# A pair with a nearly empty second block becomes a single with a small block beside it

## The chip, the cores and the metric

One core of a Trainium2 chip runs the whole program in one launch. The metric is device time in microseconds (us), median of the runs. Engines: PE (matrix), DVE (vector), ACT (activation), POOL (GpSimd; it issues the indirect gathers and scatters), SP (issues the plain DMAs). PE's weight loads are listed as PEld.

## The reference, cut to what matters

```
a = attention(q, k, v)              # 4 batches, 8 heads, 768 positions, window plus block summaries
x = a as 3072 tokens of 512 numbers
g_idx = argmax(x @ w_group)         # 4 groups
e_idx = argmax(xg @ w_expert[g])    # 4 experts in the group: 16 experts, one for each token
for each expert with tokens:
    h  = relu(xe @ w1[g, e])        # 512 -> 1024
    ye = h @ w2[g, e]               # 1024 -> 512
    out[tokens] = (g_weight * e_weight)[:, None] * ye
```

Counted from the reference on the given inputs, experts 0 to 15 get 0, 203, 922, 118, 0, 1445, 0, 4, 1, 0, 0, 0, 0, 379, 0 and 0 tokens. In blocks of 128: expert 1 two (128 and 75 tokens), expert 2 eight (the last has 26), expert 3 one (118), expert 5 twelve (the last has 37), experts 7 and 8 one each (4 tokens and 1), expert 13 three (the last has 123).

## The kernel before, in words

**Stages.** Attention runs first and writes x to DRAM. Beside it the Router works out each token's expert and place. Four full blocks of the expert that leads after two batches ("first", here expert 5) run while the router finishes; their work is `first`. All other blocks become units, and the unit tables are made on the chip by `units`, `unit_rows` and `unit_slots` while `first` runs: `units` turns the counts per expert into the number of pairs, singles ("ones") and tiny units and their first row; `unit_rows` writes the table of the unit's expert (SP reads it to load weights); `unit_slots` builds one-hot columns (`eq`, `bo`), multiplies them on PE, and writes the table of token numbers, `t_unit_gather`, which POOL's gathers read.

**A planner sets the order** of the router's instructions among the blocks of `first`. It keeps a modelled PE clock and a modelled DVE clock; each DVE instruction is charged 85 ns (`VECTOR_NS`) and 1 ns a column, a 256-column matmul 107 ns. After each step of `first` (12 matmuls of stage 1, 6 of stage 2) it appends router instructions until the DVE clock is past the PE clock. `pause` holds a matmul back until the PE clock is ahead of the DVE clock by so many ns. What isn't appended when the last half block of `first` is to begin (tag "units") is appended there, ahead of that half block. Engines then run their queues in order.

**A unit** has two stages: x (high and low part) times w1, relu, times w2 (high and low part); three matmuls for each product in split precision. ACT writes the high parts (L1032), DVE the low ones. A `pair` has two blocks of 128 tokens of one expert and one set of weights (4 MB, SP, L1018). A `one` has one block, and a `tiny` unit at most 32 tokens, in plain fp32 on the raw weights in four column strips. Two pairs are certain, further pairs are nested `If`s (L1302). Then come the ones, nested (L1311), and behind each `one(i)` the `tiny(i)` if there is one (L1315). For the counts above that makes ten pairs, two ones (experts 3 and 13) and two tiny units (7 and 8).

**Around a one.** At its start POOL gathers the tokens of tiny unit i+1 and of the one after next, then drains; SP loads the next one's weights and those of the tiny unit. `x_t_tiny(i)` (L1208) transposes the tiny tokens in the second stage of `one(i)`: PE executes it in order. Scatters to `out` go out in order on POOL, each waiting for the one before it.

**A skipped `If`.** Each engine branches by itself. Where the body is skipped, an engine that has instructions in it runs one semaphore instruction in its place, which waits until the engine's own earlier instructions are done and raises its semaphore by what the body would have raised.

Of the kernel before, what the change touches and what calls it, by code (L numbers as in the profile page):

```python
# [8 lines left out]
F32 = mybir.dt.float32  # L9
F32R = mybir.dt.float32r  # L10
BF16 = mybir.dt.bfloat16
I32 = mybir.dt.int32
# [8 lines left out]
P = 128  # L21
# [19 lines left out]
NONE = E  # L41
TINY = 32
NTINY = E // 2
SLOTS = 2 * NPAIR + NONE + NTINY
# [25 lines left out]
AHEAD, LATE_AHEAD, SLOT_AHEAD, VECTOR_NS = 300, 1500, 800, 85  # L70
# [64 lines left out]
class Router:  # L135
# [3 lines left out]
    def __init__(self, tc, pool, ps, ident):  # L139
# [16 lines left out]
        for name, rows, n in (("first", 1, 1), ("unit", 32, 3), ("count", 1, 3), ("next", 32, 1)):  # L156
            t[name] = pool.tile([rows, n], I32, name="t_" + name)
# [216 lines left out]
    def slots(self, name, col, nt, step, c0):  # L374
# [5 lines left out]
        eqs = [self.tile("eq_%s%d" % (name, j0), step, n) for j0 in groups]  # L380

        def columns(values):
# [3 lines left out]
            for j0, eq in zip(groups, eqs):  # L386
# [8 lines left out]
                yield from self.pause(SLOT_AHEAD)  # L395
# [49 lines left out]
    def units(self):  # L445
# [18 lines left out]
        un = self.tile("un", 3, E)  # L464
        V.tensor_copy(out=un, in_=bi)
        yield

        V.scalar_tensor_tensor(out=un[:, 2], in0=un[:, 2], scalar=1.0, in1=un[:, 1], op0=ALU.is_equal, op1=ALU.mult)
        yield
        start = self.start = self.tile("ustart", 3, E)  # L470
        for a, z in ((0, 2), (2, 3)):
            before = self.tile("look", 2, E, E)[:, 0:z - a]
            V.tensor_tensor(out=before, in0=self.lower[:, None].broadcast_to([P, z - a, E, E]),
                            in1=un[:, a:z, None, :].broadcast_to([P, z - a, E, E]), op=ALU.mult)
            yield
            V.reduce_sum(out=start[:, a:z], in_=before, axis=AX.X)
            yield
        end = self.end = self.tile("uend", 3, E)
        V.tensor_tensor(out=end, in0=start, in1=un, op=ALU.add)
        yield  # L480


        large = self.tile("ularge", 1)
        V.tensor_tensor(out=large, in0=end[:, 1, E - 1:E], in1=end[:, 2, E - 1:E], op=ALU.subtract)
        yield
        V.scalar_tensor_tensor(out=un[:, 2], in0=start[:, 2], scalar=large, in1=un[:, 2], op0=ALU.is_lt, op1=ALU.mult)
        yield
        below = self.tile("ubelow", E)
        V.tensor_scalar(out=below, in0=start[:, 2], scalar1=large, scalar2=None, op0=ALU.min)
# [3 lines left out]
        V.tensor_tensor(out=start[:, 1], in0=start[:, 1], in1=below, op=ALU.subtract)  # L493
        yield
        V.tensor_tensor(out=end[:, 1:3], in0=start[:, 1:3], in1=un[:, 1:3], op=ALU.add)
# [7 lines left out]
        V.tensor_tensor(out=ut[:, 2], in0=start[:, 2], in1=start[:, 1], op=ALU.subtract)  # L503
        yield
        V.scalar_tensor_tensor(out=ut[:, 2], in0=ut[:, 2], scalar=float(NONE), in1=un[:, 2], op0=ALU.add, op1=ALU.mult)
        yield
        V.tensor_tensor(out=ut[:, 2], in0=ut[:, 2], in1=start[:, 1], op=ALU.add)
# [437 lines left out]
class Experts:  # L945
# [11 lines left out]
    def tiles(self, pool, early):  # L957
# [17 lines left out]
        else:  # L975
# [6 lines left out]
            self.xTt, self.wt = pool.tile([P, KC, TINY], F32, name="xt"), pool.tile([P, 1], F32, name="wt")  # L982
# [11 lines left out]
    def col(self, row, half=0):  # L994
        name, i = row
        if name == "first":
            return name, i
        return "unit", dict(unit=2 * i + half, one=2 * NPAIR + i, tiny=2 * NPAIR + NONE + i)[name]
# [121 lines left out]
    def pair(self, i):  # L1120
# [39 lines left out]
    def one(self, i):  # L1160
# [10 lines left out]

        def h_t(n):
# [10 lines left out]
        if 0 < i < NTINY:  # L1183
            for which in range(2):
                self.load_w(("tiny", i), which, self.n_tiny > i)
        for n in range(2):
# [11 lines left out]
            self.nc.scalar.activation(out=self.xg2[0][:, n], in_=hp, func=AF.Relu)  # L1198
        load(1)
# [245 lines left out]
```

## Time and profile before

| what | value |
|---|---|
| time, median of 3 runs | 524.16 us (523.22 to 525.19) |
| the profiled execution's own time | 524.9 us |
| its span, first to last instruction | 523.1 us |
| PE busy / PE weight loads busy | 94% / 80% |
| DVE / ACT / POOL busy | 69% / 61% / 23% |
| granted PE clock, mean | 0.989 |
| DMA, mean over the span | 204 GB/s |

Busy shares are averages over stages with different limits: attention up to about 190 us, `first` and the tables up to about 241 us, pairs up to 478 us, then ones and tiny units to 515 us. In a timeline row the first number is the start, the second the time in us, and in brackets stands how long the engine was idle before it and what ended that.

### The profile page before, as it was taken

How to read it: one execution, taken by the hardware profiler on the slowest of the kernel's cores; microseconds unless marked ns; L12 is line 12 of the kernel's file. 1: busy time of each engine (PE TensorE's matmuls, PEld its weight loads, DVE VectorE, ACT ScalarE, POOL GpSimd, SP SyncE). 2: the span in 40 equal slices, each digit the busy share in tenths (PEclk: the TensorE clock that was granted, in tenths of full speed). 3: DMA queues.
4: the chain of work that ended last, by engine and by line, in shares of the span. 5: the costliest groups of instructions: out<-in, count | busy, mean ns of one | idle time of the engine just before them, and what ended most of it. 6: DMA issues, size and time to landing. Idle time of an engine off the chain costs nothing.

```text
span 523.1 us, 13329 instructions
## 1 busy us (share of the span) xinstructions
PE 493.3 (94%) x4966; PEld 418.1 (80%) x4966; DVE 359.7 (69%) x1090; ACT 316.8 (61%) x595; POOL 121.1 (23%) x200
## 2 busy tenths in 40 slices
PE   7799999999999789989999999999999999999993
PEld 4677767776777688969898989899898989897782
DVE  7787899888887878876755547473746546473782
ACT  5599888888989642216645546463645546474681
POOL 7322113111313400045020202022121302023222
PEclk9799999999999999999999999999999999999998
DMA  9999766967757530196996665655566666653890
GB/s 169 181 185 179 159 150 186 182 140 212 167 136 254 173 113 21 48 366 214 404 370 243 243 234 196 250 222 186 200 222 230 244 236 202 256 203 134 283 355 29
DMA packets 72501, 106.95 MB, mean 204 GB/s; under 512 B 40286, under 2 KB 40366, under 8 KB 68576
## 3 DMA queue, kind: packets, MB, share of 16 engines
q1 hardware_dynamic: 67456, 90.98, 59.6%
q0 software_dynamic: 4960, 14.92, 7.8%
q8 instruction: 43, 0.70, 0.6%
q14 instruction: 42, 0.34, 0.3%
HBM read 97.49 MB, written 13.24 MB: 212 GB/s over the span
## 4 chain that ended last, share of the span: by engine, by line
PE 55%; issue 16%; DVE 13%; DMA 10%; ACT 2%; POOL 2%; POOLq 1%; ACTq 0%; DVEq 0%
PE ps_s L120 32%; PE ps_av L120 11%; PE ps_tr L120 11%; DMA out_dram<-y,t_unit_scatter 4%; DVE ss L794 3%; DMA x_dram<-xt 2%; DVE ks L774 2%; DMA xg<-x_dram,t_first_gather 1%; DVE kw L763 1%; DMA xd<-x_dram,t_unit_gather 1%; ACT kw L763 1%; PE ps_lg L658 1%; DVE kw L771 1%; POOLq L1181 1%; POOL out_dram L1078 1%
## 5 line engine op out<-in xcount | busy, mean ns | idle before, releaser
L120 DVE TENSOR_TENSOR w2l<-w2r,w2h 128x1024 fp32r<-128x1024 f32 x52 | 63.4, 1226 | 77.2 <-ACT w2h L1032 76.8
L120 PE MATMUL ps_s<-xT,w1h 128*128 128x256 f32 x448 | 83.6, 285 | 0.0
L120 PEld LDWEIGHTS ps_s<-xT,w1h 128*128 128x128 f32 x448 | 70.8, 192 | 0.9 <-issue 0.6
L1078 POOL DMA_INDIRECT out_dram<-y,t_unit_scatter x24 | 25.8, 1074 | 195.8 <-ACT y L1073 110.3
L120 PE MATMUL ps_s<-xT,w1l 128*128 128x256 f32 x224 | 63.4, 283 | 0.0
L803 ACT ACTIVATE pr<-ss,nm 128x120 f32<-128x120 f32 x192 | 60.1, 387 | 4.7 <-DVE nm L794 4.3
L1116 ACT ACTIVATE hTh<-ps_s 128x512 fp32r<-128x512 f32 x48 | 28.7, 597 | 56.4 <-PE ps_s L120 35.9
L737 POOL COPY va<-vr 24x256 f32<-24x256 f32 x96 | 34.7, 405 | 121.3 <-DVE vr L734 114.4
L120 DVE TENSOR_TENSOR w1l<-w1r,w1h 128x1024 fp32r<-128x1024 f32 x52 | 60.4, 1219 | 3.1 <-ACT w1h L1032 3.1
L120 PE MATMUL ps_s<-ohr,w1h 128*128 128x256 f32 x320 | 59.0, 283 | 0.0
L1032 ACT CAST w2h<-w2r 128x1024 fp32r<-128x1024 f32 x52 | 53.7, 1041 | 1.2 <-DVE lg L864 0.6
L120 DVE SCALAR_TENSOR_TENSOR hTl<-ps_s,hTh 128x512 fp32r<-128x512 f32 x48 | 33.1, 690 | 26.8 <-ACT hTh L1116 26.0
L1032 ACT CAST w1h<-w1r 128x1024 fp32r<-128x1024 f32 x52 | 50.7, 1050 | 0.0
L120 PEld LDWEIGHTS ps_s<-ohr,w1h 128*128 128x128 f32 x320 | 49.9, 188 | 0.2
L794 DVE CUSTOM_DVE_ANT_0 ss<-mask,ps_s 128x120 f32<-128x120 f32 x192 | 42.1, 274 | 4.4 <-PE ps_s L120 3.7
L120 PE MATMUL ps_s<-ohr,w1l 128*128 128x256 f32 x160 | 45.0, 281 | 0.0
L120 PE MATMUL ps_s<-kw,qt 64*64 64x120 f32 x768 | 38.0, 279 | 5.7 <-DVE nm L794 4.6
L120 PEld LDWEIGHTS ps_s<-xT,w1l 128*128 128x128 f32 x224 | 43.0, 192 | 0.3
L120 PE MATMUL ps_s<-w2h,hTh 128*128 128x512 f32 x104 | 41.7, 401 | 0.0
L120 PE MATMUL ps_av<-w2h,hTh 128*128 128x512 f32 x104 | 41.6, 400 | 0.0
L120 PE MATMUL ps_av<-w2l,hTh 128*128 128x512 f32 x104 | 41.1, 395 | 0.0
L120 PE MATMUL ps_s<-w2h,hTl 128*128 128x512 f32 x104 | 41.1, 395 | 0.0
(270 smaller groups left out, 1017.8 us busy)
## 6 DMA issues: line engine op xcount, KB each, us to landing
w2r<-in_moe_w_dram SPq DMA_DIRECT2D x32, 1024.0 KB, 5.3
w1r<-in_moe_w_dram SPq DMA_DIRECT2D x30, 1024.0 KB, 8.6
kn<-in_k_dram SPq DMA_DIRECT2D x16, 384.0 KB
qn<-in_q_dram SPq DMA_DIRECT2D x16, 384.0 KB, 5.6
va<-in_v_dram SPq DMA_DIRECT2D x32, 192.0 KB, 4.0
x_dram<-xt SPq DMA_DIRECT2D x12, 512.0 KB, 4.2
va<-in_v_dram SPq DMA_DIRECT2D x64, 44.0 KB, 5.3
w_first<-in_moe_w_dram SPq DMA_DIRECT2D x2, 1024.0 KB, 5.1
```

The lines of the kernel that those rows point to most:

```text
L120: return f(*args, **kw)
L658: nc.tensor.matmul(out=t, lhsT=zero, rhs=zero[:, None, :].broadcast_to([P, 4, P]), start=True, stop=True)
L737: nc.gpsimd.tensor_copy(out=va[KW:NC, i:i + n, :, 0:D], in_=vr[KW:NC].broadcast_to([NBLK, n, 2, D]))
L763: (nc.scalar.copy if j == 0 or h and idx in ACT_K1 else V.tensor_copy)(out=out[:, j], in_=tv.rearrange("p i t r -> p t r i"))
L771: V.tensor_copy(out=kw[:, 1:NQT, before], in_=kw[:, 0:NQT - 1, QT - PAD:QT])
L774: V.reduce_max(out=ks, axis=AX.X, in_=kw[:, :, 0:QT].rearrange("p t (a k) -> p t a k", k=BLOCK))
L794: V.tensor_tensor_reduce(out=ss[:, u], in0=mask[:, 1 if t == 0 else 2 if t == NQT - 2 else 0], in1=sp[h][:, j], scale=1.0, scalar=3.4e38, ...
L803: nc.scalar.activation(out=pr[:, i, 0:NC], in_=sp[:, i], func=AF.Exp, bias=nm[:, i:i + 1], scale=-1.0)
L1032: self.nc.scalar.copy(out=h, in_=src)
L1078: self.nc.gpsimd.indirect_dma_start(out=self.out, out_offset=bass.IndirectOffsetOnAxis(ap=self.tabs[name, "scatter"][0:y.shape[0], col:col ...
L1116: nc.scalar.activation(out=th[:, js], in_=hp, func=AF.Relu)
L1181: self.nc.gpsimd.drain()
```

## The change

A pair whose second block has at most 32 tokens is no longer a pair. It is listed as a one, behind the ones that have tiny units, and its second block as a small block `i` beside `one(i)`, which uses that one's raw weights. `tiny` is cut in two, `tiny1` (through h) and `tiny2`; beside a one, `tiny1` stands at its start and `tiny2` between its stages, each under `If`s. At most 4 units are tiny and at most 4 beside. For the counts above expert 2's fourth pair (128 and 26 tokens) qualifies: nine pairs, three ones (experts 3, 13 and 2), two tiny units, one small block beside `one(2)`.

```diff
-AHEAD, LATE_AHEAD, SLOT_AHEAD, VECTOR_NS = 300, 1500, 800, 85
+AHEAD, LATE_AHEAD, SLOT_AHEAD, WEIGHT_AHEAD, VECTOR_NS = 300, 1500, 800, 3000, 85
...
-                yield from self.pause(SLOT_AHEAD)
+                yield from self.pause(SLOT_AHEAD if values[0] is self.tok1 else WEIGHT_AHEAD)
...
     def units(self):
...
-        for a, z in ((0, 2), (2, 3)):
-            before = self.tile("look", 2, E, E)[:, 0:z - a]
-            V.tensor_tensor(out=before, ...)          # 128x512, then 128x256
-            V.reduce_sum(out=start[:, a:z], in_=before, axis=AX.X)
+        # the four counts packed into one number, 5 bits each (4 instructions)
+        V.tensor_tensor(out=before, in0=self.lower, in1=packed[:, 1:2].broadcast_to([P, E, E]), op=ALU.mult)
+        V.reduce_sum(out=packed[:, 0], in_=before, axis=AX.X)
+        # ... unpacked (4 instructions), caps, starts and ends by some 30 small ones
...
     def unit_rows(self):
-        V.tensor_copy(out=self.tabs["count"], in_=self.end[0:1, :, E - 1])
+        V.reduce_max(out=cnt[:, 0:3], in_=self.end[0:1], axis=AX.X)
+        V.tensor_copy(out=cnt[:, 3:4], in_=self.n_small[0:1])
+        V.tensor_copy(out=self.tabs["count"], in_=cnt)
...
     def pair(self, i):
                 elif i == 0 and part == 0:
                     self.x_t_one(0)
+                    self.gather(("tiny", 0), self.xg1[0][0:TINY])
+                elif i == 1 and part == 0:
+                    self.x_t_tiny(0)
...
     def one(self, i):
+        def beside(work):
+            if i < NTINY:
+                with self.tc.If(self.n_small > i):
+                    if i < NTINY - NBESIDE:
+                        with self.tc.If(self.n_tiny <= i):
+                            work()
+                    else:
+                        work()
...
-        for t in ((0, 1) if i == 0 else (i + 1,)):
-            if t < NTINY:
-                self.gather(("tiny", t), self.xg2[1][0:TINY, t % 2])
+        beside(lambda: self.tiny1(i, ("one", i)))
+        if i + 1 < NTINY:
+            self.gather(("tiny", i + 1), self.xg2[1][0:TINY, 0])
         self.gather_one(i + 2)
         self.nc.gpsimd.drain()
         load(0)
...
+        beside(lambda: self.tiny2(i, ("one", i)))
         load(1)
         for part, _ in enumerate(self.stage2(...)):
...
-            if part == 1 and i < NTINY:
-                self.x_t_tiny(i)
+            if part == 1 and i + 1 < NTINY:
+                self.x_t_tiny(i + 1)
...
     def tiny(self, i):
+        self.tiny1(i, ("tiny", i))
+        self.tiny2(i, ("tiny", i))
```

So the tokens of tiny unit i+1 are gathered at the start of `one(i)` and transposed in its second stage; before, a whole one lay between. Tiles of the small blocks move into the router's `eq` tiles, and `wt` gets two buffers.

## Rows read from the trace of the kernel before

**Rows 1.** The page: busy time by engine; the chain that ended last, by engine

```profile
PE 493.3 (94%) x4966; PEld 418.1 (80%) x4966; DVE 359.7 (69%) x1090; ACT 316.8 (61%) x595; POOL 121.1 (23%) x200
...
PE 55%; issue 16%; DVE 13%; DMA 10%; ACT 2%; POOL 2%; POOLq 1%; ACTq 0%; DVEq 0%
```

**Rows 2.** Busy time in stretches (start:end, us): two pairs, one(0), tiny(0), one(1)

```profile
283.24:306.93 23.69, 23.69 (x154) 21.49 (x153) 13.51 (x15) 12.36 (x16) 4.28 (x4) 1.00 0.60 222
306.93:330.49 23.56, 23.56 (x153) 21.37 (x153) 13.49 (x15) 12.37 (x16) 4.22 (x4) 1.00 0.62 224
...
478.74:492.26 13.52, 13.52 (x64) 10.68 (x65) 9.97 (x11) 10.41 (x13) 4.70 (x4) 1.00 0.93 330
492.26:496.83 4.57, 4.42 (x132) 3.71 (x131) 2.08 (x4) 1.23 (x3) 2.36 (x5) 1.00 0.43 119
496.83:510.26 13.43, 13.43 (x66) 10.66 (x65) 10.72 (x13) 11.16 (x15) 3.27 (x3) 1.00 0.92 348
```

**Rows 3.** PE's timeline where x_t_tiny(0) stands in one(0)

```profile
488.67 0.66 PE L120 MATMUL ps_tr<-ident,ohr 32*128 32x32 f32 x4
```

**Rows 4.** DVE's timeline while the tables are made

```profile
207.52 0.68 DVE L120 TENSOR_TENSOR look<-lower,un 128x512 f32<-128x512 f32 x1
...
213.00 0.69 DVE L120 SCALAR_TENSOR_TENSOR hTl<-ps_s,hTh 128x512 fp32r<-128x512 f32 x1 [2.23 <-ACT hTh L1116]
...
214.78 0.17 DVE L120 SCALAR_TENSOR_TENSOR ut<-ut,un 128x16 f32<-128x16 f32 x1
214.99 0.18 DVE L120 TENSOR_TENSOR ut<-ut,ustart 128x16 f32<-128x16 f32 x1
...
218.42 0.16 DVE L120 CAST t_unit<-uex 32x3 int32<-32x3 f32 x1
...
227.89 0.22 DVE L120 TENSOR_SCALAR t_unit_gather<-ps_lg 128x62 uint32<-128x62 f32 x1 [1.37 <-PE ps_lg L120]
```

**Rows 5.** POOL's timeline: the first gather of unit 0

```profile
228.38 1.22 POOL L1039 DMA_INDIRECT xd<-x_dram,t_unit_gather  x1 [16.93 <-DVE t_unit_gather L120]
```

**Rows 6.** PE's timeline: the transposes of unit 0's tokens

```profile
235.68 1.23 PE L120 MATMUL ps_tr<-ident,xd 128*128 128x128 f32 x8 [1.25 <-DMA xd<-x_dram,t_unit_gather]
```

**Rows 7.** PE's timeline: from the last pair into one(0)

```profile
477.43 0.39 PE L120 MATMUL ps_s<-w2h,hTl 128*128 128x512 f32 x1
478.74 0.50 PE L120 MATMUL ps_s<-w1h,xs 128*128 128x512 f32 x1 [0.91 <-ACT y L1073]
```

**Rows 8.** Line 1302 from 470 to 479 us: ns min/median/max, first and last start

```profile
L1302 PEldq COMPARE_BRANCH  x2: 193/2005/3817, 473.5 to 478.0; - x2
...
L1302 PEldq EVENT_SEMAPHORE  x1: 51/51/51, 477.9 to 477.9; - x1
```

**Rows 9.** Line 1315 in the whole span, the same columns

```profile
L1315 PEldq COMPARE_BRANCH  x4: 65/124/191, 488.8 to 514.1; - x4
```

**Rows 10.** ACT's timeline: tiny(0)'s output

```profile
496.92 0.74 ACT L1253 ACTIVATE y<-ps_lg,wt 32x128 f32<-32x128 f32 x2 [1.33 <-PE ps_tr L120]
```

**Rows 11.** SP's timeline: weight loads for unit 0 and in one(1)

```profile
219.76 0.99 SPq L1018 DMA_DIRECT2D w1r<-in_moe_w_dram  x2
...
493.95 2.24 SPq L1018 DMA_DIRECT2D w1r<-in_moe_w_dram  x4
```

**Rows 12.** Stretches of 2 us in one(1); the last number is the GB/s moved

```profile
501.00:503.00 2.00, 2.00 (x14) 1.78 (x13) 1.61 (x3) 1.78 (x3) 0.14 (x1) 1.00 0.98 409
...
509.00:511.00 2.00, 2.00 (x34) 1.49 (x36) 2.00 (x4) 1.33 (x2) 0.00 (x0) 1.00 0.16 51
```

**Rows 13.** POOL's timeline: gather of tiny(2) in one(1); the last scatter

```profile
504.08 1.32 POOL L1039 DMA_INDIRECT ohr<-x_dram,t_unit_gather  x1 [0.30 <-issue]
...
516.84 0.89 POOL L1078 DMA_INDIRECT out_dram<-y,t_unit_scatter  x1 [3.14 <-DMA out_dram<-y,t_unit_scatter]
```

**Rows 14.** Line 1039 from 503 to 512 us

```profile
DMA to landing us min/median/max: 5.4/5.7/6.0
```

**Rows 15.** PE's timeline: last matmuls of the program

```profile
514.55 0.28 PE L120 MATMUL ps_lg<-w2r,xd 128*32 128x128 f32 x2
```

More of the change, by code (lines that the diff above doesn't have):

```diff
@@ L43 @@
 NTINY = E // 2
+NBESIDE = NTINY // 2
 SLOTS = 2 * NPAIR + NONE + NTINY
@@ L153, in __init__ @@
         t = self.tabs = {}
-        for name, rows, n in (("first", 1, 1), ("unit", 32, 3), ("count", 1, 3), ("next", 32, 1)):
+        for name, rows, n in (("first", 1, 1), ("unit", 32, 3), ("count", 1, 4), ("next", 32, 1)):
             t[name] = pool.tile([rows, n], I32, name="t_" + name)
@@ L379, in slots @@
         groups = range(0, nt, step)
-        eqs = [self.tile("eq_%s%d" % (name, j0), step, n) for j0 in groups]
+        eqs = self.eqs = [self.tile("eq_%s%d" % (name, j0), step, n) for j0 in groups]
         def columns(values):
@@ new lines, in units @@
+        yield
+        V.tensor_tensor(out=packed[:, 1], in0=packed[:, 0], in1=packed[:, 1], op=ALU.add)
+        yield
+        whole = self.tile("uwhole", 2, E, dt=I32)
+        V.tensor_copy(out=whole, in_=packed)
+        yield
+        field = self.tile("ufield", 4, 2, E, dt=I32)
+        for i in range(4):
+            V.tensor_scalar(out=field[:, i], in0=whole, scalar1=5 * i, scalar2=31, op0=ALU.arith_shift_right, op1=ALU.bitwise_and)
+            yield
+        sf = field.bitcast(F32)
+        V.tensor_copy(out=sf, in_=field)
@@ L478, in units @@
+        yield
+        small = self.n_small = self.tile("unsmall", 1)
+        V.tensor_tensor(out=small, in0=na, in1=nb, op=ALU.add)
+        yield
+        start = self.start = self.tile("ustart", 3, E)
         end = self.end = self.tile("uend", 3, E)
-        V.tensor_tensor(out=end, in0=start, in1=un, op=ALU.add)
+        V.scalar_tensor_tensor(out=un[:, 3], in0=s_b, scalar=float(NBESIDE), in1=un[:, 3], op0=ALU.is_lt, op1=ALU.mult)
         yield
-        large = self.tile("ularge", 1)
-        V.tensor_tensor(out=large, in0=end[:, 1, E - 1:E], in1=end[:, 2, E - 1:E], op=ALU.subtract)
+        V.scalar_tensor_tensor(out=un[:, 2], in0=s_a, scalar=cap, in1=un[:, 2], op0=ALU.is_lt, op1=ALU.mult)
@@ new lines, in units @@
+        yield
+        V.tensor_tensor(out=start[:, 1], in0=s_o, in1=start[:, 2], op=ALU.subtract)
+        yield
+        V.tensor_tensor(out=un[:, 0], in0=un[:, 0], in1=un[:, 3], op=ALU.subtract)
+        yield
+        rest = self.tile("urest", 1, E)
+        V.tensor_scalar(out=rest[:, 0], in0=start[:, 1], scalar1=na, scalar2=nb, op0=ALU.is_ge, op1=ALU.mult)
+        yield
+        V.tensor_tensor(out=start[:, 1], in0=start[:, 1], in1=rest[:, 0], op=ALU.add)
+        yield
+        V.scalar_tensor_tensor(out=rest[:, 0], in0=s_b, scalar=na, in1=start[:, 1], op0=ALU.add, op1=ALU.subtract)
@@ L490, in units @@
+        yield
+        V.tensor_tensor(out=rest[:, 0], in0=rest[:, 0], in1=un[:, 3], op=ALU.mult)
+        yield
+        V.tensor_tensor(out=start[:, 1], in0=start[:, 1], in1=rest[:, 0], op=ALU.add)
         yield
@@ L492, in units @@
         yield
-        V.tensor_tensor(out=start[:, 1], in0=start[:, 1], in1=below, op=ALU.subtract)
+        V.tensor_tensor(out=un[:, 1], in0=un[:, 1], in1=un[:, 3], op=ALU.add)
         yield
-        V.tensor_tensor(out=end[:, 1:3], in0=start[:, 1:3], in1=un[:, 1:3], op=ALU.add)
+        V.tensor_tensor(out=end, in0=start, in1=un[:, 0:3], op=ALU.add)
         yield
@@ L997, in col @@
             return name, i
-        return "unit", dict(unit=2 * i + half, one=2 * NPAIR + i, tiny=2 * NPAIR + NONE + i)[name]
+        return "unit", dict(unit=2 * i + half, one=2 * NPAIR + min(2 * i, i + NTINY), tiny=2 * NPAIR + 2 * i + 1)[name]
     def bank(self, name, i):
```

106 lines of the change are left out of this document (72 added, 34 removed).

## The prediction

> **What bounds the kernel now.** I read the busy shares and the chain first [rows 1]: PE is busy 94% of the span and holds 55% of the chain, and the chain names lines, not stages. So I went to busy time by stretch [rows 2]: in a pair PE is busy for all of its 23.69 or 23.56 us while DVE and ACT need 13.5 and 12.4, so a pair is worth its PE time, 23.62 us, and everything else in it is hidden. A one is full of PE work too, 13.52 and 13.43 us, but DMA is at 330 to 348 GB/s there against 222 in a pair, and a tiny unit adds 4.57 us. Two places are bound otherwise. Ahead of pair 0, PE idles 1.25 us until unit 0's gathered tokens land [rows 6], and that gather hangs on the token table that DVE finishes at 228.1 us [rows 4, 5]; a later table is a later pair 0, and as pairs have no slack the whole rest moves with it. And at the exit from the pairs, where a branch is not taken, PE idles 0.91 us [rows 7].
>
> **The change part by part.** The sum is made against the profiled execution (524.9 us, span 523.1; 0.7 us above the median of 524.16), and I move the difference onto the median.
>
> *One pair less:* expert 2's eighth block has 26 tokens, so ten pairs become nine: -23.62 us [rows 2].
>
> *One one more:* +13.45 us, the mean of the two shown [rows 2]. The small block beside it does on PE what a tiny unit does, 64 matmuls, four transposes, 64 matmuls, 4.57 us, no weights of its own; taken branches are prepared while PE works off its queue (65 to 191 ns [rows 9]), I add 0.1. Together +18.1 us. If the one's stage 1 covers tiny2's wait for hT, it is 0.2 less.
>
> *x_t_tiny* now also runs in pair 1 and for i+1 in every one: four times in place of two, one of which is inside the added one. The other is +0.6 us in pair 1 (its transposes show 0.66, some of it the matmul before running out [rows 3]), on PE, which has no slack there. Its gather and its POOL copies are hidden by a pair's length.
>
> *The tables, later.* In `units`, behind the cast of `un`, stood 20 DVE instructions: 16 small ones, a multiply and a sum over 512 columns (0.68 each [rows 4]) and the same over 256 (about half). Now there are 44, two over 256 columns and 42 small; `unit_rows` gets two more. So +28 small ones and -1.3 us of large ones. A small one that needs the one before it starts 0.21 us after it (214.78 to 214.99 [rows 4]); where the planner interleaves it with another chain it costs half that. Lower end 28 x 0.1 - 1.3 = 1.5 us, upper end 28 x 0.21 - 1.3 = 4.6. The cover is DVE's idle time of 2.23 us ahead of hTl at 213.0 [rows 4]. Following the planner's charges (101 ns a small instruction, 2.8 us more, 1.2 us less for the 512-column ones), only some 0.5 us of the new work gets in front of that hTl; the rest lies behind, in a chain of dependent instructions. I take 3.1 us for the table at 227.89. The same walk puts the last of the four groups of slot matmuls, and with it the gather, behind the tag "units"; POOL then has the scatter of `first`'s third block ahead of the gather (one issue of about 1.2 us as in [rows 5], part of it waiting time anyway), and the unit's weights, loaded from 219.76 on when the expert table of 218.42 is out [rows 4, 11], start about 3.7 us later and are still moving when the gather does. For both I add 0.8. Pair 0 starts 3.9 us later (1.5 to 5.5).
>
> *The four skips.* one(0) and one(1) have tiny units, so `beside` is skipped twice in each: at the start and between the stages. The trace of before shows no such skip inside a one. Its nearest row is the exit from the pairs: PE's semaphore instruction of the skipped body ran at 477.9 [rows 8], right behind the end of the last matmul (477.43 + 0.39 [rows 7]), and the next matmul started at 478.74, 0.92 us after that end. So a skip drains PE. Matmuls of 512 columns start every 0.23 us though each shows 0.39, so a drain also loses the overlap of 0.16. Between the stages: 0.16 and about 0.7 for the semaphore and two jumps, 0.85 each. At the start of one(0) PE stands already; only the added jumps count, 0.7. At the start of one(1) stage 1 overwrites a bank that ACT reads in the skipped body, so PE waits for ACT's own skip, and ACT is at tiny(0)'s output until 497.66 [rows 10], where stage 1 began at 496.83: 1.0. Queued behind PE's wait is the one itself. Sum 0.7 + 0.85 + 1.0 + 0.85 = 3.4 us; below, 0.1 each as a taken branch [rows 9], 0.4; above, 0.92 and 0.2 each, 4.5. I take 3.4.
>
> [...]
>
> *Gather and weights in one(1).* x_t_tiny(2) now reads a gather issued in the same one. POOL gets to that gather at 504.08, since the scatters before it wait for each other [rows 13], and it lands 5.4 to 6.0 us later [rows 14], at about 510. x_t_tiny of one(1) stood at 506.6 and comes at 510.0 with the skips: a stall of 0.3 (0 to 1.5). SP's load of w1 of the next one, the first two of the four issues at 493.95 [rows 11], moved nothing before; now it puts 2.1 MB ahead of tiny(1)'s 4.2 MB, at 409 GB/s at most [rows 12] 5.2 us, and starts up to 1.5 later with the skips of one(0). tiny(1)'s weights were in by about 510.3 [rows 12], now between 515.5 and 517, and its second half, which began at 512.9, would begin at 516.6 with what is above. So 0.4 (0 to 1). Sum 0.7 us. w2 of the next one follows by about 522, when that one is in its first stage: hidden.
>
> *The end.* Before, the last scatter of 32 rows starts 2.0 us after the last matmul, held by the scatter before it [rows 13, 15]. Now a scatter of 128 rows that is held by nothing, and one more skip on POOL. I take +0.1 (-0.7 to +1).
>
> Sum: -23.6 + 18.1 + 0.6 + 3.9 + 3.4 + 0.7 + 0.1 = +3.2 us. That is 528.1 us for the profiled execution, 527.4 at the median. WEIGHT_AHEAD is costed at nothing: for units the weight columns come behind the tag, where the clock stops nothing; for `first` it shifts some small instructions by up to one attention step, and the last attention steps keep DVE from being idle (bounds -0.5 to 1.0).
>
> **The rivals.**
>
> *The tables aren't late (not slower).* The place is DVE between 207 and 228 us. Were the added instructions taken into the 2.23 us of idle time, and the rest interleaved at 0.1 us, the table would be at most 0.5 us later, and PE's 1.25 us wait [rows 6] would hardly grow. Price: -3.7, so 523.7 us. For it: DVE does idle there [rows 4]. Against it: the idle time sits in front of an instruction that the planner puts early, and the added chain is serial. It decides below some 1.5 us of delay.
>
> *Neither delay (faster).* If besides the tables the skips cost a branch each, the sum is 527.4 - 3.7 - 3.0 = 520.7; weights of tiny(1) would then be waited for, some 1.5 us more: 522.2 at most. Only the exit from the pairs speaks against it, and there a wait for ACT ended the idle time [rows 7].
>
> *A skip jumps out of the code that PE has at hand.* The one far jump on PE that a row shows took 3817 ns, against 65 for others [rows 8, 9]. A `beside` body is some 140 instructions on PE, and the ones get longer. One such miss costs 3.75 us: 531.2. Against it: the exit jumps over eight pairs of some 300 instructions each, this one over one body. [...]
>
> *It doesn't do what it says.* If no pair qualified, ten pairs stay and the tables, skips and x_t_tiny are added: 524.16 + 3.9 + 3.4 + 0.6 = 532.1. The count of 26 tokens speaks against it.
>
> **How the numbers follow.** Forecast 0.47, tables not late 0.22, neither delay 0.16, a far jump 0.1, no pair 0.05. A measurement of this kernel tells 0.5%, 2.6 us, from no change: 521.5 and 526.8. The forecast's own range, from its bounds, is 524.5 to 530, of which some seven tenths count as slower: 0.33, with the last two 0.48. Same: 0.12 from the forecast, 0.19 from the tables' rival, 0.03 from the one with neither delay, 0.34. Faster: 0.02, 0.03 and 0.13, 0.18. The range for 8 in 10 is 521 to 531.5.
>
> **What would show it.** Nine pairs and three ones: 44 of the hTh pieces of 128x512 that pairs and first blocks make, against 48. The first xd gather on POOL about 3.5 to 4 us later than 228.4, pair 0 the same. Between the stages of one(0) and one(1) a PE gap of 0.85 us each, and one of about 1 us ahead of one(1). A wait of PE on a gather or on w2r in one(1) or tiny(1). one(2) about 18 us long. If xd's gather starts before 230 us, the tables' step is wrong; if there are no gaps in the ones, that of the skips; if the time is under 524.5, at least one of the two.

## The result, and the profile after

The changed kernel takes 529.67 us (median of 14 runs, 527.14 to 531.24); the kernel before, beside it on the same chip, 524.35 us (14 runs, 522.92 to 526.67). The ratio is 1.0086, 95% interval 1.0068 to 1.0104: about 4.5 us slower (5.3 us between the medians). 527.4 us was forecast, 521 to 531.5 the range. The profiled execution took 528.26 us with a span of 526.5 us, 3.4 us above the 523.1 us of before.

PE's share hardly moved, though a whole pair went; in the chain, DMA doubled [rows 1]. The page:

```profile
PE 491.7 (93%) x5012; PEld 413.5 (79%) x5012; DVE 361.3 (69%) x1119; ACT 316.9 (60%) x597; POOL 130.3 (25%) x208
...
PE 58%; DMA 20%; DVE 14%; issue 4%; ACT 2%; POOL 1%; POOLq 0%; DVEq 0%; ACTq 0%; SPq 0%
...
L1174 ACT ACTIVATE hTh<-ps_s 128x512 fp32r<-128x512 f32 x44 | 26.3, 597 | 52.2 <-PE ps_s L121 34.2
```

The 44 pieces of hTh are those of nine pairs: the change does what it says. To see where the time went, follow the places that the prediction named. First the tables, on DVE [rows 4]:

```profile
200.66 0.27 DVE L121 TENSOR_REDUCE mx<-lg 128x30 f32<-128x120 f32 x1
...
213.40 0.69 DVE L121 SCALAR_TENSOR_TENSOR hTl<-ps_s,hTh 128x512 fp32r<-128x512 f32 x1 [1.90 <-ACT hTh L1174]
...
222.43 0.16 DVE L121 CAST t_unit<-uex 32x3 int32<-32x3 f32 x1
...
230.72 0.22 DVE L121 TENSOR_SCALAR t_unit_gather<-ps_lg 128x62 uint32<-128x62 f32 x1 [0.37 <-PE ps_lg L121]
```

The first of these, an instruction of the router's last block that the change does not touch, stood at 200.26 before. So 0.40 us was lost ahead of the change; across the profiles of this study that instruction begins anywhere from 199.12 to 203.78 us. In the profile after, TensorE's granted clock is 0.50 from 178 to 180 us, in the attention stage, and in that of before 1.00; what makes it differ no run shows. From here I count from that instruction, the router mark. The idle time that was to take up new work only fell from 2.23 to 1.90 us; the expert table (t_unit) is 3.6 us later, the gather table 2.4 us. POOL then has the scatter ahead of the gather, as foreseen [rows 5]:

```profile
230.72 0.98 POOL L1136 DMA_INDIRECT out_dram<-y,t_first_scatter  x1 [18.87 <-ACT y L1131]
232.01 1.35 POOL L1097 DMA_INDIRECT xd<-x_dram,t_unit_gather  x1 [0.30 <-DVE bo_unit L121]
```

On PE's timeline: unit 0's tokens [rows 6], the last matmul of the last pair and the first of one(0) [rows 7], the middle of one(0), and the same two places of one(1):

```profile
239.09 1.34 PE L121 MATMUL ps_tr<-ident,xd 128*128 128x128 f32 x8 [0.25 <-DMA xd<-x_dram,t_unit_gather]
...
458.18 0.39 PE L121 MATMUL ps_s<-w2h,hTl 128*128 128x512 f32 x1
460.06 0.47 PE L121 MATMUL ps_s<-w1h,xs 128*128 128x512 f32 x1 [1.49 <-PEq L1237]
...
467.21 0.50 PE L121 MATMUL ps_av<-w2h,hTh 128*128 128x512 f32 x1 [0.42 <-ACT xT L1108]
...
479.81 0.50 PE L121 MATMUL ps_s<-w1h,xT 128*128 128x512 f32 x1 [1.00 <-ACTq L1237]
...
486.92 0.50 PE L121 MATMUL ps_s<-w2h,hTh 128*128 128x512 f32 x1 [0.42 <-ACT xs L1108]
```

Line 1237 is the branch around the block beside. Each skip shows as a gap (ahead of one(0) there were 0.91 us before, in the other three places none), and each gap is where it was expected. What was not expected at this size is in tiny(1): PE stands three times for weights, 2.8 us in all.

```profile
494.95 1.52 PE L121 MATMUL ps_s<-w1r,eq_unit 128*32 128x128 f32 x48 [0.37 <-DMA w1r<-in_moe_w_dram]
...
497.75 0.30 PE L121 MATMUL ps_lg<-w2r,eq_unit 128*32 128x128 f32 x2 [0.54 <-DMA w2r<-in_moe_w_dram]
...
500.28 0.30 PE L121 MATMUL ps_lg<-w2r,eq_unit 128*32 128x128 f32 x2 [1.89 <-DMA w2r<-in_moe_w_dram]
```

The loads behind that are on SP [rows 11], and by stretches of 2 us the transfers stay full until 504 us, ten us behind the end of one(1); before, they had run dry by its end [rows 12]:

```profile
479.09 3.13 SPq L1076 DMA_DIRECT2D w1r<-in_moe_w_dram  x4
482.81 11.06 SPq L1076 DMA_DIRECT2D w2r<-in_moe_w_dram  x4
```

The first of them, the third single's, starts 0.72 us ahead of one(1); the same place was 2.88 us ahead of it before. SP's waits (us in total, times, longest) show what holds it, first before (490 to 496 us), then after (474 to 480 us):

```profile
SPq L1018 <- DVE w1l L120: 6.1, 1, 6.1
...
SPq L1076 <- DVE w1l L121: 6.3, 1, 6.3
SPq L1076 <- PEq L1237: 3.0, 1, 3.0
```

The block beside reads the raw weights of its single. So the next load into that buffer waits until PE has passed the branch, though the body is skipped. The stretches of 2 us:

```profile
496.00:498.00 2.00, 1.30 (x32) 0.75 (x23) 0.52 (x2) 0.27 (x1) 1.04 (x2) 1.00 1.04 386
502.00:504.00 2.00, 2.00 (x65) 1.61 (x57) 0.85 (x3) 0.95 (x3) 0.22 (x1) 1.00 1.01 389
504.00:506.00 2.00, 1.85 (x9) 1.49 (x9) 0.39 (x3) 1.40 (x3) 1.52 (x2) 1.00 0.19 68
```

And the end is better than before: the last scatter waits for no other scatter [rows 13], and 5.4 us after its start the program is over; it had taken 6.3.

```profile
521.11 1.47 POOL L1136 DMA_INDIRECT out_dram<-y,t_unit_scatter  x1 [4.51 <-ACTq L1407]
```

Stage by stage, from the same marks on PE in the profiled executions (us; nsl is e_no_skip_load; the marks are the first matmuls of the stages):

| from, to | before | after | none_beside | tables | no_skip | no_load | nsl |
|---|---|---|---|---|---|---|---|
| router mark, unit 0's tokens | 35.42 | 38.43 | 38.63 | 40.63 | 39.02 | 38.49 | 38.62 |
| to one(0) | 243.06 | 220.97 | 244.78 | 242.94 | 220.52 | 221.73 | 220.67 |
| one(0) | 13.52 | 14.17 | 14.18 | 13.54 | 13.53 | 14.18 | 13.52 |
| tiny(0), to one(1) | 4.57 | 5.58 | 5.58 | 4.51 | 4.51 | 6.37 | 4.51 |
| one(1) | 13.43 | 14.13 | 14.14 | 13.43 | 18.53 | 14.21 | 15.75 |
| tiny(1), to the block | - | 7.85 | - | - | 4.54 | 4.49 | 5.14 |
| tiny(1), to the end | 12.84 | 32.56 | 12.27 | 12.82 | 29.56 | 29.65 | 31.75 |

### The profile page after: what moved, and what is told of

Same layout as the page of the kernel before. It is cut to its first block, busy times and chain, and to the rows that moved or that the text cites. A ratio compares the mean times of both kernels' runs of the same rounds, so it can differ in the third digit from the quotient of the medians.

```text
span 526.5 us, 13630 instructions
## 1 busy us (share of the span) xinstructions
PE 491.7 (93%) x5012; PEld 413.5 (79%) x5012; DVE 361.3 (69%) x1119; ACT 316.9 (60%) x597; POOL 130.3 (25%) x208
## 4 chain that ended last, share of the span: by engine, by line
PE 58%; DMA 20%; DVE 14%; issue 4%; ACT 2%; POOL 1%; POOLq 0%; DVEq 0%; ACTq 0%; SPq 0%
PE ps_s L121 34%; PE ps_av L121 13%; PE ps_tr L121 10%; DMA xg<-x_dram,t_unit_gather 7%; DMA out_dram<-y,t_unit_scatter 4%; DMA va<-in_v_dram 3%; DVE ss L852 2%; DMA x_dram<-xt 2%; DVE ks L832 2%; DMA xg<-x_dram,t_first_gather 2%; DMA xd<-x_dram,t_unit_gather 1%; DVE kw L821 1%; ACT kw L821 1%; DVE hTl L121 1%; PE ps_lg L121 1%
## 5 line engine op out<-in xcount | busy, mean ns | idle before, releaser
L1136 POOL DMA_INDIRECT out_dram<-y,t_unit_scatter x24 | 28.0, 1166 | 184.0 <-ACT y L1131 93.6
L1174 ACT ACTIVATE hTh<-ps_s 128x512 fp32r<-128x512 f32 x44 | 26.3, 597 | 52.2 <-PE ps_s L121 34.2
L121 PE MATMUL ps_s<-ohr,w1h 128*128 128x256 f32 x256 | 47.2, 283 | 0.0
L121 DVE SCALAR_TENSOR_TENSOR hTl<-ps_s,hTh 128x512 fp32r<-128x512 f32 x44 | 30.3, 690 | 24.4 <-ACT hTh L1174 24.4
L121 PE MATMUL ps_av<-w2h,hTl 128*128 128x512 f32 x104 | 41.1, 395 | 0.0
L121 PEld LDWEIGHTS ps_s<-ohr,w1h 128*128 128x128 f32 x256 | 39.9, 188 | 0.2
L121 PE MATMUL ps_s<-w2h,hTh 128*128 128x512 f32 x96 | 39.2, 409 | 0.4 <-ACT xs L1108 0.4
L121 PE MATMUL ps_s<-w2l,hTh 128*128 128x512 f32 x96 | 38.3, 399 | 0.0
```

The costliest lines, as they stand in the source:

```text
L121: return f(*args, **kw)
L1136: self.nc.gpsimd.indirect_dma_start(out=self.out, out_offset=bass.IndirectOffsetOnAxis(ap=self.tabs[name, "scatter"][0:y.shape[0], col:col ...
L1174: nc.scalar.activation(out=th[:, js], in_=hp, func=AF.Relu)
```

## The experiments

Theory: the 3.4 us are later tables, four passed branches and a wait for weights, set against a pair that is 23.6 us and a single with its block that is 18.1. Rivals: one of these is not a cost of its own; TensorE's granted clock; instruction fetch. All ratios are to the kernel before.

**Only the overheads.** No expert qualifies, the rest of the changed kernel stays:

```
-V.scalar_tensor_tensor(out=un[:, 3], in0=un[:, 2], scalar=1.0, in1=un[:, 3], op0=ALU.is_equal, op1=ALU.mult)
+V.scalar_tensor_tensor(out=un[:, 3], in0=un[:, 2], scalar=9.0, in1=un[:, 3], op0=ALU.is_equal, op1=ALU.mult)
```

> The changed kernel, but the test for a small second block compares with 9 in place of 1, so that no expert qualifies: ten pairs, two singles and two tiny units run as in the kernel before, under the changed tables and branches. Theory: only the overheads stay, the later tables (+3.4 us at pair 0) and four passed branches (+2.75 us); the wait of the second tiny unit for its weights goes, since no third single loads beside it, and the end is again held by the last scatter. Sum +6.1 us over the kernel before, ratio 1.0117. Rival: what the change costs lies in the new single and its block, then the overheads come to 2 us or less (ratio 1.004). Rival 2: TensorE's granted clock, which the changed kernel has at 0.5 from 235 to 239 us, costs beside the wait for the tables: then over 7.5 us (ratio above 1.014).

531.24 us, ratio 1.0104 (1.0052 to 1.0157): 5.5 us, 6.1 expected. The table shows it in place: 3.2 at unit 0's tokens, 1.7 up to one(0), 0.66, 1.01 and 0.71 in one(0), tiny(0) and one(1), 0.57 less at the end. That is 6.7 us from a router mark that came 1.1 us sooner than before. The 1.7 us are the skip (0.58), x_t_tiny in pair 1 (24.34 us in place of 23.56) and 0.36 between unit 0's tokens and the first matmul of pair 0, where the granted clock is still below 1.00 (0.61 from 235 to 240 us). So the overheads are real, and the rival that lays the cost on the new single falls. The interval reaches 8.2 us and does not exclude the clock's rival; in this trace the clock's part is some 0.6 us, 0.2 ahead of unit 0's tokens and the 0.36 behind them.

**The later table by itself.** In the kernel before:

```
+more = self.tile("umore", E)
+V.tensor_copy(out=more, in_=start[:, 0])
+yield
+for _ in range(26):
+    V.tensor_scalar_add(more, more, 0.0)
+    yield
+V.tensor_copy(out=start[:, 0], in_=more)
+yield
 ut = self.tile("ut", 3, E)
```

> The kernel before with 28 more small dependent instructions on VectorE in the chain of the unit tables (a copy, 26 additions of zero, a copy back), nothing else. Theory: they take 28 x 0.11 = 3.1 us, nothing absorbs them but 0.3 us, and pair 0 begins later by 2.8 to 3.4 us; ratio 1.0055 to 1.0065. Rival 1: VectorE's idle of 2.23 us ahead of the table and the transfers of weights behind it take most of it up, and the time grows by less than 1 us. Rival 2: the idle of TensorE that this opens lowers its granted clock, as in the changed kernel between 234 and 239 us, and the time grows by over 4 us.

531.01 us, ratio 1.0121 (1.0086 to 1.0156), twice what was expected. The dose was larger: in DVE's timeline 13 dependent instructions take 2.69 us, 0.21 us each as in [rows 4], and not 0.11:

```profile
216.28 2.69 DVE L120 TENSOR_SCALAR umore<-umore 128x16 f32<-128x16 f32 x13
218.88 0.68 DVE L120 SCALAR_TENSOR_TENSOR hTl<-ps_s,hTh 128x512 fp32r<-128x512 f32 x1
```

From the router mark the expert table came 6.8 us later, the gather table 4.2, the transposes of unit 0's tokens 5.2, and every stage behind them took what it takes in the kernel before (table). But the clock, rival 2, has a part in the 5.2. The granted clock is 0.56 from 235 to 240 us and 0.76 from 240 to 245, and PE is busy with the slot matmuls and the last ones of `first` up to the transposes, without a wait for the tokens:

```profile
235.09 5.09 PE L120 MATMUL ps_lg<-bo_unit,ohr 128*128 128x124 f32 x24 [1.35 <-DVE bo_unit L120]
...
242.56 1.12 PE L120 MATMUL ps_tr<-ident,xd 128*128 128x128 f32 x8
```

The gathers, issued at 234.27 and 235.80 us, landed 6.1 to 6.2 us later, the first at about 240.4, 2 us before PE came to it. So up to 2.1 of the 5.2 us are the clock's and at least 3.1 the table's. In the changed kernel the expert table is 3.6 us later and the tokens are 3.0, and there PE does wait for the tokens (0.25 us), so the gather bounds it. Most of the table's delay was a delay of the program in both, and no stage behind pair 0 gave any back; the time of this run alone would not have told the table from the clock.

**The planner's allowance.** WEIGHT_AHEAD back at 800.

> The changed kernel with the planner's allowance for the columns of the weights back at 800 ns in place of 3000. Theory: it moves only the order of TensorE's work in the last first-expert stage; pair 0 waits for the gather of its tokens in either case, so the time stays within 1 us. Rival: the larger allowance is what keeps TensorE from standing still for the later tables; without it the time grows by 1 to 3 us. Rival 2: the larger allowance itself delays pair 0 (TensorE waits 1.35 us for the weights' columns at 232 us), then 1 us or more is gained.

530.34 us, ratio 1.0105 (1.0066 to 1.0144), not to be told from the changed kernel; the gather table is 30.07 us behind the router mark, against 30.06. It is worth nothing either way. Its profile also shows how much two executions can differ: from the router mark to the end it is 3.3 us longer than the changed kernel's. Pair 0 begins 1.0 us later, with the granted clock at 0.50 from 235 to 240 us, and tiny(1) and the block beside take 2.3 us more, with PE waiting 1.07 and 1.25 us for DVE and the clock at 0.70 from 500 to 505 us, behind a wait for weights of 1.59 us.

**No passed branches.**

```
-if i < NTINY:
+if i == 2:
     with self.tc.If(self.n_small > i):
```

> The changed kernel, but the small block beside a single is built for the third single alone, so that no branch around it is passed over in the first two singles (right for these inputs only, where the one small block goes with the third single). Theory: the four passed branches cost what the trace of the changed kernel shows at them, 0.57 and 0.59 us in the first single, 1.0 and 0.59 us in the second, together 2.75 us; so about 2.7 us less than the changed kernel, some 1.0034 of the kernel before where the changed kernel has 1.0086. Rival 1: the gaps are there anyway (before the change the first single already began after 0.91 us of idle), and next to nothing goes (0 to 0.7 us). Rival 2: instruction fetch, the blocks that are built but jumped over make later branches long, and more goes (over 3.5 us).

529.74 us, ratio 1.0078 (1.0044 to 1.0111): hardly less than the changed kernel, as rival 1 said, but for another reason. By the trace the four gaps do go: 0.45 ahead of one(0), 0.64 in it, 1.07 ahead of one(1), 0.59 in it to its second layer, together 2.75 us, so the passed branches are their cause. The third single's load starts 2.78 us ahead of one(1) again, and tiny(1) waits for no weights (4.54 us). But one(1) takes 18.53 us, 4.4 more than in the changed kernel: PE waits 3.53 us for its tiny gather, and behind that wait the granted clock is at 0.50, where the matmuls of 512 columns start every 0.43 us in place of 0.23, which is 1.6 us more:

```profile
494.04 0.64 PE L121 MATMUL ps_tr<-ident,ohr 32*128 32x32 f32 x4 [3.53 <-DMA ohr<-x_dram,t_unit_gather]
...
496.00:498.00 2.00, 2.00 (x7) 1.54 (x6) 1.27 (x2) 0.00 (x0) 0.53 (x3) 0.50 1.00 385
```

POOL shows why the gather is late:

```profile
478.13 1.04 POOL L1136 DMA_INDIRECT out_dram<-y,t_unit_scatter  x1 [0.15 <-issue]
486.99 0.90 POOL L1136 DMA_INDIRECT out_dram<-y,t_unit_scatter  x1 [7.82 <-DVE w2l L121]
488.19 0.99 POOL L1097 DMA_INDIRECT ohr<-x_dram,t_unit_gather  x1 [0.30 <-issue]
```

In the changed kernel the second scatter went 4.2 us after the first and the gather at 481.74. There the first scatter landed after 2.7 us, before the loads at 479.09; here the loads start at 477.83, while it is under way, it lands after 8.0 us, and it is 8.9 us until the second may follow, and the gather behind it. (The row names a cast on DVE as what ended the wait; the second scatter's own data were there by 481.6 us.) From unit 0's tokens to the end the trace is 0.76 us shorter. So 2.0 of the 2.75 us were given back: the wait for the gather and the low clock behind it (5.1 us) stand where the wait for weights (3.3 us) stood. Rival 2, instruction fetch, by which over 3.5 us go, is not borne out.

**Taking the transfers away.** The third single's weights are not loaded:

```
-if i + 1 < NONE:
+if i + 1 < NONE and i != 1:
     self.load_w(("one", i + 1), which, self.n_ones > i + 1)
```

> The changed kernel without the loads of the third single's two matrices (4 MB in the second single; the third single computes with what the buffers hold), all else as it is. Theory: with 4 MB in place of 8 MB from 479 us on, the second tiny unit's weights and the tiny gather come in time, the waits of 2.8 us in the second tiny unit go, and the time falls by 2.8 us or, with a fall of TensorE's granted clock that such a wait brings in some runs, by up to 6 us (ratio to the kernel before 0.999 to 1.0033, where the changed kernel has 1.0086). Rival: the waits are of another cause (the order of the queue, the branches), and the time falls by less than 1 us.

527.25 us, ratio 1.0062 (1.0041 to 1.0083). By medians 2.4 us less than the changed kernel; by ratios 1.3, with intervals that overlap. The trace is clearer: no wait for weights is left, and tiny(1) takes 4.49 us in place of 7.85. That the third single's 4 MB cause tiny(1)'s wait is shown. Some of the gain went again: 0.8 us at tiny(0), where PE waits 0.49 and 0.39 us for DVE, and 0.8 us between unit 0's tokens and the first matmul of pair 0, where the granted clock is 0.50 from 235 to 240 us.

> The changed kernel without the loads of the third single's matrices (as e_no_load) and with the small block built for the third single alone (as e_no_skip). Theory: in e_no_skip the 2.75 us of the passed branches were won and given back to the waits behind the full transfers; with the transfers relieved both gains stay, 2.75 us below e_no_load and 5.5 us below the changed kernel (ratio 0.994 to 0.998). Rival: the branches give nothing even so, and the time is that of e_no_load within 1 us.

(Both edits.) 528.88 us, ratio 1.0100 (1.0071 to 1.0129), no better than without the second edit: the rival's case. one(1) starts 3.6 us sooner, counted from unit 0's tokens, and the end comes at the same time. The first 1.5 us go to the tiny gather again, though fewer weights move; it stands behind two scatters on POOL, the second 8.6 us after the first (the table's column nsl). Another 1.5 us go to PE's waits for DVE in tiny(1) and in the block beside (0.76 and 1.23 us).

```profile
490.70 0.64 PE L121 MATMUL ps_tr<-ident,ohr 32*128 32x32 f32 x4 [2.29 <-DMA ohr<-x_dram,t_unit_gather]
```

So once the branches are gone the next thing late is POOL's queue: scatter, its landing, scatter, gather, with the third single's weights or without them.

**Loading sooner or later.** Two edits of the order on SP:

```
 # e_early_w1, at the end of one(i) in place of the start of one(i + 1)
+if i + 2 < NONE:
+    self.load_w(("one", i + 2), 0, self.n_ones > i + 2)
 # e_late_w2: load(1) behind the second layer
```

> The changed kernel, but the first matrix of a single's expert is loaded at the end of the single two before it (for the third single: after the first single, ahead of the first tiny unit), not at the start of the single before it. Theory: the second tiny unit waits 0.37 + 0.54 + 1.89 = 2.8 us for its weights because 2 MB of the third single stand ahead of them in the same queue, while the transfers rest from 474 to 480 us; so the three waits go, and the time falls by 2.8 us (ratio to the kernel before 1.0033). Rival: the transfers are the bound over this stretch (8 MB at about 390 GB/s), the wait comes back at the third single's second matrix, and the time falls by less than 1 us.

531.57 us, ratio 1.0111 (1.0059 to 1.0164). The load was not early: SP reached it at 472.7 us and stood at it until 479.63, 6.9 us of it for DVE's split of the weights in that buffer, and the wait for the tiny gather came instead, 4.44 us, with the granted clock at 0.50 from 498 to 502 us. It tests nothing but that the program's order does not set the time of this load.

```profile
479.63 0.34 SPq L1076 DMA_DIRECT2D w1r<-in_moe_w_dram  x1
```

> The changed kernel, but the second matrix of the next single's expert is loaded after the second layer of a single, not ahead of it. Theory: the second tiny unit waits for its weights (0.37 + 0.54 + 1.89 us) because 2 MB of the third single's second matrix, issued at 486.6 and 490.4 us, share the transfers (about 400 GB/s, full from 481 to 503 us) with them; issued later they give way, the waits go or shrink under 0.5 us, and the time falls by 2 to 2.8 us (ratio to the kernel before 1.0035 to 1.005 where the changed kernel has 1.0086). Rival: the transfers are simply full, and the wait moves to the third single's second matrix: less than 1 us is gained.

535.14 us, ratio 1.0171 (1.0127 to 1.0215): the slowest but for e_tiny_first and its bare form, and it does not test its theory. The third single's second matrix hardly moved: SP issued it 6.8 and 9.1 us behind one(1)'s first matmul, in the changed kernel 6.8 and 10.6, since SP runs ahead of the singles and the buffers, not the place in the program, set the time. tiny(1) still waits 0.41 and 1.97 us for its second matrix, and which of the third single's two matrices holds it up stays open. Then more is lost: behind the wait the granted clock is 0.50 for some 7 us, and DVE comes to the block beside 5.20 us after its last work, 2.8 of them with PE waiting. What held DVE the trace does not name ("remote"); that stays open.

```profile
498.00:500.00 2.00, 0.65 (x16) 0.41 (x16) 0.00 (x0) 0.07 (x1) 0.05 (x1) 0.96 1.07 396
500.00:502.00 2.00, 1.26 (x24) 1.18 (x28) 0.00 (x0) 0.00 (x0) 0.00 (x0) 0.50 1.04 402
```

```profile
509.61 0.29 DVE L121 TENSOR_SCALAR eq_unit<-ps_s 128x128 f32<-128x128 f32 x1 [5.20 <-remote]
```

**Four rearrangements for a faster kernel.** In the first two the next gathers and the second matrix are issued at the end of a single; e_as_tiny also makes the small block a tiny unit of its own (in part):

```
-        self.gather_one(i + 2)        # and the tiny gather, at the start of one(i)
+        load(1)                       # at the end of one(i)
+        gathers(i + 1)
 # e_as_tiny: no beside(); behind one(i)
-                        with tc.If(self.n_tiny > i):
+                        with tc.If(self.n_small > i):
```

> The changed kernel with the small block built for the third single alone (as in e_no_skip), with the next single's second matrix loaded after the second layer (as in e_late_w2), and with the gathers that a single issues at its start issued at the end of the single before it, while the transfers rest. Theory: without the passed branches the singles ran 2.75 us sooner in e_no_skip, and 2 us of that were lost again because the third tiny gather stood 3.53 us behind the weights; fed earlier, both gains stay: 2.75 + 2.8 = 5.5 us less than the changed kernel, about the time of the kernel before (ratio 0.998 to 1.000). Rival: the stretch from the second single on is bound by its 8 MB of weights whatever their order, and less than 3 us is gained (ratio above 1.003).

> The changed kernel, but a small second block is run as one more tiny unit behind its single, with its expert's weights loaded once more as a tiny unit's (4 MB more for the one block here), so that no branch for it stands inside a single; two more small instructions in the tables; gathers and second matrices fed as in e_no_skip_feed. Theory: the four passed branches (2.75 us) and the wait for weights (2.8 us) go, two instructions cost 0.25 us, and the end is again held by the last tiny unit's scatter behind the single's (1.8 us more): 3.5 us less than the changed kernel, ratio 1.001 to 1.003. Rival: the 4 MB more come late for the last block, since the tiny buffers are free only after the second tiny unit (502 us), and the block waits 2 us or more: ratio above 1.005.

531.01 us, ratio 1.0125 (1.0094 to 1.0157), and 529.55 us, ratio 1.0085 (1.0057 to 1.0114): neither gains. The gather now comes in time, but the weights then move during tiny(0), at 377 to 418 GB/s from 478 to 480 us, and PE stands in it three times for some 0.3 us with nothing named but "issue". In e_as_tiny tiny(0) takes 6.77 us up to one(1) where e_no_skip has 4.51. The stops shown are 0.9 of these 2.3 us; between them PE's weight loads stand 0.57 to 0.59 us at a time. Whether that is instruction fetch, the third rival, was not tested:

```profile
478.46 0.33 PE L121 MATMUL ps_tr<-w2r,eq_unit 128*32 128x128 f32 x2 [0.29 <-issue]
479.22 0.30 PE L121 MATMUL ps_lg<-w2r,eq_unit 128*32 128x128 f32 x2 [0.32 <-issue]
479.98 0.29 PE L121 MATMUL ps_tr<-w2r,eq_unit 128*32 128x128 f32 x1 [0.33 <-issue]
```

The last two put the small unit of one(i) at its start and load the next tiny weights from there (in part):

```
 def small():
     if i < NTINY:
         with self.tc.If(self.n_small > i):
+            with self.tc.If(self.n_tiny > i) as tiny:   # _bare: if i < 2 / else, when built
+                self.tiny(i)
+            with tiny.Else():
+                self.tiny1(i, ("one", i)); self.tiny2(i, ("one", i))
```

> The changed kernel with the small work of a single, tiny unit or small block, in one place at its start under one branch with an else-part, the next tiny unit's weights loaded from the single before it on (460 us in place of 479). Theory: the second tiny unit's weights have 20 us and more to come, so its 2.8 us of waiting go; of the four passed branches the two in mid-single go (1.2 us), those at the start stay (0.6 and 1.0 us): 4 us less than the changed kernel, ratio 1.000 to 1.002. Rival: the 4 MB that now move in the first single come together with the second single's 4 MB and delay those: a wait of 2 us or more in the second single, ratio above 1.005.

> As e_tiny_first, but with tiny units built for the first two singles and the small block for the third alone, so that nothing is passed over (right for these inputs only). Theory: 1.5 to 2 us less than e_tiny_first, ratio 0.996 to 0.999, the first version below the kernel before. Rival: what the branches cost is hidden by transfers that are late anyway, and the time is that of e_tiny_first within 0.7 us.

540.59 us, ratio 1.0302 (1.0272 to 1.0331), and 536.67 us, ratio 1.0229 (1.0201 to 1.0257): far off. A cause that neither theory nor rival had named shows in the bare one. The tiny unit's output now follows a single's or pair's output at once, and waits for the scatter that still reads its buffer of two:

```profile
470.68 0.74 ACT L1346 ACTIVATE y<-ps_lg,wt 32x128 f32<-32x128 f32 x2 [5.99 <-DMA out_dram<-y,t_unit_scatter]
```

Behind it ACT's casts and the single's relu are late (PE waits 3.45 us). The two kernels differ by 3.9 us, the branches and the else-part, twice what the theory gave them; in e_tiny_first PE also stands 5.73 us ahead of one(1) with nothing named, which stays open. No kernel of these beats the one before.

## Why the prediction was right, and where it was not

The total was right, and so was the mechanism of the larger terms: a pair is worth its PE time, a single and its block cost theirs, the tables come late and the skips leave gaps. The sizes of two smaller terms were wrong, and they cancel. The sum of terms was 3.2 us; the profiled execution shows 3.4, of which 0.4 lie ahead of the change. Term by term:

- *A pair for a single.* -23.6 + 18.1 + 0.6 forecast. From unit 0's tokens to the last pair's last matmul it is 219.09 us against 241.75, -22.7 with x_t_tiny in it (-23.0 forecast; x_t_tiny made pair 1 0.79 us longer, not 0.6). From tiny(1) to the end the program got 19.7 us longer; without the wait (3.4 us, of 7.85 for a period of 4.5) and the gain at the end (1.8) that is 18.2. Right. (The mean of the two singles is 13.48 and not 13.45, which changes nothing.)
- *Tables.* 3.9 forecast, 3.0 measured from the router mark: the gather table 2.4 us later where 3.1 was forecast, the rest the scatter that POOL has ahead of the gather. The chain was serial as argued, and only 0.3 us of the idle time took up work. e_tables shows that a longer chain alone delays pair 0, though part of its delay is the clock's. The rival by which the tables are not late is out.
- *Skips.* 3.4 forecast; 0.57 + 0.59 + 1.00 + 0.59 = 2.75 measured, in each of the four places (2.9 by the stages in the table). e_no_skip shows that the passed branches are the cause. That the drain and not the branch instruction is the price is argued from the sizes: the trace shows the branch itself at 67 to 333 ns and the gaps at 0.6 to 1.0 us.
- *Gather and weights.* 0.7 forecast; 2.8 of idle time measured, 3.4 by the length of tiny(1), beyond the 2.5 that the two upper bounds made together. This is the term that was mis-sized. I had let the loads start up to 1.5 us later; counted from one(1)'s first matmul they started 2.2 us later (0.72 us ahead of it, where it was 2.88 before [rows 2, 11]), though that matmul itself comes 1.0 us later by the skip. One step that failed is that a skip was priced on PE alone: SP waited 3.0 us more for PE to pass it, as the block beside reads the buffer that the load fills. In e_no_skip that wait is gone and the load is 2.78 us ahead. But 0.7 us more delay than allowed does not make all of the excess. The prediction also counted 6.3 MB up to tiny(1)'s last weights and took the third single's second matrix as hidden; from 478 to 500 us some 7.5 MB moved. e_no_load shows that the third single's 4 MB cause the wait; how the excess divides no run separates. The split was also wrong: all of it fell on the weights, none on the gather, and e_no_skip shows that the two change places.
- *The end.* +0.1 forecast, from -0.7 up. It is -1.8: from the last output on ACT (520.14) to the end of the span it is 6.4 us against 8.2 (514.92 before). About half is the scatter's start, 1.05 us after the last matmul in place of 2.0 [rows 13, 15]: the wait for the scatter before is gone, which I had seen but had set against a skip on POOL. The other half is from the last scatter's start to the end, 5.4 us in place of 6.3; I had taken that as fixed, and no run shows what shortened it.

The last two are wrong by +2.7 and -1.9 us, the tables and the skips by -0.9 and -0.5, and they cancel; that the total came within 0.2 us is in part luck. The prediction did say, under its second rival, that weights would be waited for once the skips went, "some 1.5 us more"; in e_no_skip 2.0 of the 2.75 us were given back, to the gather and the low clock behind its wait.

*A far jump.* The long branch is still at the exit from the pairs, once, as before [rows 8], and the skips in the singles show none:

```profile
L1394 PEldq COMPARE_BRANCH  x9: 65/65/3707, 288.7 to 458.8; - x9
...
L1237 PEldq COMPARE_BRANCH  x12: 67/176/333, 459.3 to 512.2; - x12
```

*The runs against the profile.* The 14 runs are slower by 4.5 us (ratio) or 5.3 us (medians), the profile by 3.4. It is the fourth fastest of the 14 and one of two at the highest mean granted clock, 0.986; the others go down to 0.972, and spans of 529 us and more stand at 0.977 or less. So the 1 to 2 us go with stretches of low clock that differ between runs. In or behind a wait for weights or a gather one shows in e_late_w2, e_wa800, e_no_skip and e_early_w1, and one ahead of pair 0 in every trace with the later table. The prediction had no term for the clock. How much belongs to the change and how much to the attention stage was not separated.

## What to carry to other kernels

A unit that is cheaper on the bounding engine can bring transfers of its own, and where the others in that stretch already run at 330 to 348 GB/s [rows 2] and full stretches show some 400 (386 to 408 from 494 to 504 us in the changed kernel), time saved ahead of it comes back as a wait for them: price a change by what arrives when, and look again after each stall that you remove. A branch whose body is skipped left PE idle for 0.6 to 1.0 us here; count it by where the engines stand, not by the branch, and ask which buffers the skipped body reads, since their next load waits for the branch too (3.0 us on SP here). And a serial chain of small instructions ahead of the first gather of a full pipeline is paid for the most part (3.0 us at the tokens for 3.6 in the chain): shorten it before adding to it.

## What the hardware showed that was not expected

- The granted clock. Before, it is 1.00 in all stretches from 225 to 260 us. In the changed kernel and in all twelve experiments it falls for some us between 230 and 245 us, to 0.50 from 236 to 238 us in the changed kernel and to 0.50 to 0.61 in the lowest 5 us of each experiment, behind waits for the later table (in the changed kernel PE idle 0.63, 0.53, 0.38 and 1.35 us between 226 and 232; the wait of 1.35 us is in all thirteen traces, and not in that of before). e_tables shows that the later table alone brings it. The profiles after and before:

```profile
235.00:240.00 5.00, 4.75 (x18) 3.84 (x19) 2.57 (x9) 0.12 (x1) 3.56 (x3) 0.66 1.02 388
...
236.00:238.00 2.00, 2.00 (x6) 1.63 (x7) 1.45 (x9) 0.00 (x0) 1.70 (x2) 0.50 1.04 418
```

```profile
235.00:240.00 5.00, 4.32 (x22) 3.70 (x23) 3.56 (x5) 3.54 (x5) 2.36 (x3) 1.00 0.67 199
```

In the profile after, this cost little, since unit 0's tokens landed after the slow matmuls (PE idle 0.25 us ahead of their transposes); in e_none_beside there was no idle time left there, and the tokens' transposes came 0.2 us later; in e_tables it cost up to 2.1 us.

- Dependent instructions of 16 columns on DVE start 0.21 us apart (e_tables, as in [rows 4]), though each only adds zero.
- A scatter of a whole block holds the next one on POOL, by the order that the program gives them, and each gather behind that: for 4.2 us while the transfers rest (the changed kernel), and beside weights for 8.6, 8.9 and 9.8 us (e_no_skip_load, e_no_skip and e_no_load).
